# Two chunks of an attention-plus-MLP kernel share each half of the weights, with partial sums in a DRAM scratch

## The chip, the cores and the metric

The kernel runs on one core of a Trainium2 chip. The metric is the device time of one execution in microseconds (us), the median of several runs; lower is better. Engines are named as in the profile: PE (matrix products), PEld (its weight loads), DVE (VectorE), ACT (ScalarE), POOL (GpSimd), SP (SyncE, which issues nearly all DMAs here).

## The reference

Attention with a causal window of 128 keys and 4 sink keys, over 4 batches, 8 heads, 768 positions and 64 channels a head; then a two-layer MLP with a squared ReLU over the 3072 resulting rows of 512 channels:

```python
scores = q @ k.T / sqrt(64)
keep = (pos_k < n_sink) | ((rel >= 0) & (rel < window))     # rel = pos_q - pos_k
a = softmax(where(keep, scores, -1e9)); x = a @ v           # heads side by side: 3072 x 512
r = maximum(x @ w_in, 0)                                    # w_in 512 x 2048
out = (s * (r * r) + b) @ w_out                             # w_out 2048 x 512, float32
```

## The kernel before

*Chunks and weights.* The 3072 rows are cut into eight chunks of 384 rows (half a batch each), taken in the order 0, 2, 1, 3, 4, 5, 6, 7. The 2048 hidden columns are cut into 16 "weights" of 128 columns: `weight[f]` holds the slice of `w_in` and of `w_out` that belongs to them. Products are done in a rounded 32-bit format in three parts: high x high, high x low, low x high. So every operand is split into two halves, and each product is three matmuls.

*The MLP of one chunk* (`moe_steps`) is a list of steps. `l1(f)` multiplies x by the first half of weight f (12 matmuls into one PSUM tile `h`, L569), takes the ReLU on ACT (L572), squares and scales on DVE (L573), and splits the result into the high part (ACT, L575) and the low part (DVE, L576) of a tile `g`, of which there are three buffers. `l2(f)` multiplies `g` by the second half (nine matmuls, L587) and adds into three PSUM tiles `po`, one for each 128 rows, which stay open for all 16 weights. Step `l2(f)` stands two weights behind `l1(f)`. After the last weight ACT scales each `po` into an `ot` tile (L591), and SP stores it (L684).

*Attention for the next chunk* is cut into slots that are dealt out evenly over the steps of the current chunk. For the chunks that stand first in their batch's order (chunk 0, and chunk 2 as the second) the slots come from `plain_slots`: 24 units of scores (L474), row maximum (L481), exponent (L487), normalisation (L494 to L497), transposes (L509), product with v (L522), and the split of x into two tiles (L525, L526). For the others they come from `attn_slots`, which uses `hl` tiles (two buffers, one for each head in flight), `xm` tiles and sink corrections; its last unit writes x at L384 and L385. x has two buffers.

*Making the weights.* The weights arrive as raw 32-bit pairs of 1 MB a weight (L172), or in two pieces (the last weights: L172 and L180), and are turned into the high and low halves by stages: two ACT passes (L199, L200), two DVE passes (L201, L202) and one POOL addition (L204), then an ACT copy (L209), and a subtraction on DVE or, for each fourth weight, on POOL (L215). The raw pieces of the very last weight lie in two buffers of `g`. `weights(n_load, n_make)` issues loads and stages up to a given number; there are 33 stages. A function `before` calls it ahead of each `l1(f)` of the first chunk, with two stages for each weight.

The instructions of all engines are put into order by a scheduler, in which the order of writing is the priority: an instruction that is ready can be placed ahead of an earlier one that is not. Dependencies between tiles are followed by the framework.

Of the kernel before, what the change touches and what calls it, by code (L numbers as in the profile page):

```python
# [6 lines left out]
F32 = mybir.dt.float32  # L7
# [5 lines left out]
ALU = mybir.AluOpType  # L13
AX = mybir.AxisListType

P = 128
B, H, S, D = 4, 8, 768, 64
NS = 16
BLK = 3
CH = BLK * P  # L20
DM = H * D
DFF = 2048
NCC = DM // P
NF = DFF // P
# [3 lines left out]
WUP = 256.0  # L28
LOADS = 8
SMB, HLB = 4, 2  # L30
# [4 lines left out]
ORDER = 0, 2, 1, 3, 4, 5, 6, 7  # L35
LB, LC, LD, L2 = 2, 4, 1, 2
# [3 lines left out]
def tile_kernel(ctx, tc, qT, kT, k0, v, vsk, n_sink, window, w, s, b, out):  # L40
    nc = tc.nc
# [5 lines left out]
    def ps(name):  # L47
        return psA.tile([P, 512], F32, tag="a", name=name)

    wk_cm = tc.tile_pool(name="wk", bufs=2)  # L50
    wk = wk_cm.__enter__()
# [170 lines left out]
    def new_chunk(c):  # L222
        k = Chunk()
        k.c, k.b, k.half = c, c // 2, c % 2
        k.x = [wk.tile([P, NCC, CH], F32R, tag=f"x{i}", name=f"x{i}_{c}") for i in range(2)]
        k.cc, k.xx, k.heads, k.pairs = {}, {}, {}, {}
        return k
# [145 lines left out]
    def unit_d(k, h, i):  # L373

        if h % 2 == 1 and i == BLK - 1:
            pr = h // 2
            pp = k.pairs[pr]
            os_ = ps("os")
            nc.tensor.matmul(os_[:, :CH], pp.vs, pp.xs, start=True, stop=True)
            zb = ps("zb")  # L380
            nc.tensor.matmul(zb[:, :CH], sel, pp.xs, start=True, stop=True)
            nc.vector.tensor_tensor(out=pp.x, in0=os_[:, :CH], in1=pp.x, op=ALU.add)
            nc.vector.tensor_tensor(out=pp.x, in0=zb[:, :CH], in1=pp.x, op=ALU.mult)
            nc.scalar.copy(k.x[0][:, pr, :], pp.x)  # L384
            nc.gpsimd.tensor_tensor(out=k.x[1][:, pr, :], in0=pp.x, in1=k.x[0][:, pr, :].bitcast(F32), op=ALU.subtract)  # L385

    def attn_slots(c):
        k = new_chunk(c)
        units, ahead = [], {}
        for pr in range(H // 2):  # L390
            h, t0 = 2 * pr, 2 * BLK * pr
            units += [(h + hh, i) for hh in range(2) for i in range(BLK)]
            todo = ((-5, load_pair, pr), (-5, load_keys, h), (-2, load_sinks, pr), (-2, prep_head, h), (-2, load_keys, h + 1),
                    (1, prep_head, h + 1))
            for d, fn, a in todo:
                ahead.setdefault(max(t0 + d, 0), []).append((fn, a))
        n = len(units)

        def slot(t):
            def f():  # L400

                for fn, a in ahead.get(t, ()):
                    fn(k, a)
                if t < n:
                    unit_a(k, *units[t])
                if 0 <= t - LB < n:
                    unit_b(k, *units[t - LB])
                if 0 <= t - LC < n:
                    unit_c(k, *units[t - LC])
                if 0 <= t - LC - LD < n:  # L410
                    unit_d(k, *units[t - LC - LD])
            return f

        return k, [slot(t) for t in range(n + LC + LD)]
# [140 lines left out]
        return k, [slot(t) for t in range(n + lc)]  # L555


    def moe_steps(x, store, wk, before=None, last=False):
        g = {}
        po = [None] * BLK  # L560

        def l1(f):
            if before:
                before(f)
            h = ps("h")
            i = 0
            for cc in range(NCC):
                for wi, xi in ((0, 0), (0, 1), (1, 0)):
                    nc.tensor.matmul(h[:, :CH], weight[f][:, 0, wi, cc * P:(cc + 1) * P], x[xi][:, cc, :], start=(i == 0), stop=(i == 11))  # L569
                    i += 1  # L570
            r = wk.tile([P, CH], F32, tag="r", name="r", bufs=RB)
            nc.scalar.activation(r, h[:, :CH], AF.Relu, scale=1.0 / WUP)  # L572
            nc.vector.scalar_tensor_tensor(out=r, in0=r, scalar=s_ap, in1=r, op0=ALU.mult, op1=ALU.mult)  # L573
            gg = wk.tile([P, 2, CH], F32R, tag="g", name="g", bufs=3)
            nc.scalar.activation(gg[:, 0, :], r, AF.Identity, bias=b_ap, scale=1.0)  # L575
            nc.vector.scalar_tensor_tensor(out=gg[:, 1, :], in0=r, scalar=b_ap, in1=gg[:, 0, :].bitcast(F32),  # L576
                                           op0=ALU.add, op1=ALU.subtract)
            g[f] = gg

        def l2(f):  # L580
            gg = g.pop(f)
            for tb in range(BLK):
                if f == 0:
                    po[tb] = psO.tile([P, DM], F32, tag="po", name="po")
                tsl = slice(tb * P, (tb + 1) * P)
                for i, (gi, wi) in enumerate(((0, 0), (0, 1), (1, 0))):
                    nc.tensor.matmul(po[tb], gg[:, gi, tsl], weight[f][:, 1, wi, :],  # L587
                                     start=(f == 0 and i == 0), stop=(f == NF - 1 and i == 2))
                if f == NF - 1:
                    ot = wk.tile([P, DM], F32, name="ot", **(dict(tag="hl", bufs=HLB) if last and tb < 2 else dict(tag="ot")))  # L590
                    nc.scalar.mul(ot, po[tb], 1.0 / WUP)  # L591
                    store(tb, ot)

        steps = []
        for f in range(NF + L2):
            if f < NF:
                steps.append(lambda f=f: l1(f))
            if f >= L2:
                steps.append(lambda f=f: l2(f - L2))
        return steps  # L600

# [79 lines left out]
    def store_at(c):  # L681
        def f(tb, ot):
            r0 = c * CH + tb * P
            nc.sync.dma_start(out[r0:r0 + P, :], ot)  # L684
        return f
# [3 lines left out]
    def weights(n_load, n_make):  # L689
        while made[0] < min(n_make, 2 * NF + 1):  # L690
            while made[0] // 2 >= loaded[0] and loaded[0] < NF:
                load_weight(loaded[0])
                loaded[0] += 1
            make_weight(made[0])
            made[0] += 1

        n_wide = NF - NARROW - 1
        while loaded[0] < min(n_load, NF) and (loaded[0] < n_wide or made[0] > 2 * n_wide - 2):
            load_weight(loaded[0])
            loaded[0] += 1  # L700

    def before(f):
        weights(f + 2 + LOADS // 2, 2 * f + 5)

    def out_of_range():

        bad = const.tile([P, 4], F32, tag="bad", name="bad")
        nc.vector.tensor_reduce(out=bad[:, 0:1], in_=negm, axis=AX.X, op=ALU.max)
        nc.vector.tensor_scalar(out=bad[:, 0:1], in0=bad[:, 0:1], scalar1=0.9e9, scalar2=None, op0=ALU.is_ge)
        tc.keep_in_program_order(nc.vector.tensor_scalar(out=bad[:, 1:2], in0=n_ap, scalar1=float(NS), scalar2=None, op0=ALU.is_gt))  # L710
        nc.vector.tensor_scalar(out=bad[:, 2:3], in0=w_ap, scalar1=float(P), scalar2=None, op0=ALU.is_gt)
        nc.vector.tensor_scalar(out=bad[:, 3:4], in0=w_ap, scalar1=1.0, scalar2=None, op0=ALU.is_lt)
        bad1 = const.tile([P, 1], F32, tag="bad1", name="bad1")
        nc.vector.tensor_reduce(out=bad1, in_=bad, axis=AX.X, op=ALU.max)
        cnt = ps("cnt")
        nc.tensor.matmul(cnt[0:1, 0:1], bad1, one, start=True, stop=True)
        flag = const.tile([1, 1], I32, tag="flag", name="flag")
        nc.vector.tensor_copy(flag, cnt[0:1, 0:1])
        go = nc.values_load(flag, min_val=0, max_val=P)
        return go  # L720

    NC_ = 2 * B
    k, slots = plain_slots(0)
# [8 lines left out]
    first_cm.__exit__(None, None, None)  # L732
    late_cm = tc.tile_pool(name="late", bufs=1)
    late.append(late_cm.__enter__())
    for j, c in enumerate(ORDER):
        steps = moe_steps(k.x, store_at(c), wk, before if j == 0 else None, j == NC_ - 1)
        slots = []
        if j + 1 < NC_:
            k, slots = (plain_slots if j == 0 else attn_slots)(ORDER[j + 1])
        i = 0  # L740
        for n, st in enumerate(steps):
            st()
            if j == NC_ - 1 and n == NF // 2:
                go = out_of_range()
            while i < len(slots) and i * len(steps) < (n + 1) * len(slots):
                slots[i]()
                i += 1

    late_cm.__exit__(None, None, None)
    wk_cm.__exit__(None, None, None)  # L750
    with tc.If(go > 0):
# [46 lines left out]
```

## Time and profile before

| what | value |
|---|---|
| time of three runs | 775.47, 776.76, 777.45 us; median 776.76 |
| the profiled execution | 775.64 us, of which the span of instructions is 773.9 |
| PE busy | 733.9 us, 95% of the span |
| PE weight load, DVE, ACT, POOL busy | 85%, 64%, 62%, 31% |
| mean granted PE clock | 0.989 |
| read from and written to DRAM | 45.88 MB and 6.29 MB |

A busy share is the time in which an engine had an instruction running. DVE's and POOL's instructions can also be busy while they wait for memory. A view by windows gives the busy time of each engine in stretches of the span, a view by lines groups instructions of one source line, engine and shape, with their mean duration and with what ended the idle time ahead of them.

### The profile page before, as it was taken

What the parts mean: (1) busy time and instruction counts of PE and PEld (TensorE: products, weight loads), DVE (VectorE), ACT (ScalarE), POOL (GpSimd) and SP (SyncE); (2) the same over time, 40 slices, a digit from 0 to 9 for tenths busy, and PEclk for the clock granted to TensorE, in tenths of its full rate; (3) what the DMA queues carried; (4) which work ended last, traced back from release to release, by engine and by line L of the source; (5) the groups of instructions that cost most, each with busy time, mean ns of one, the idle gap of its engine ahead of it and who ended that gap; (6) DMA issues with size and microseconds to landing.
All of it is one profiled execution on the core that took longest, in us unless ns stands there. A gap on an engine that the chain in (4) does not pass through costs nothing.

```text
span 773.9 us, 11988 instructions
## 1 busy us (share of the span) xinstructions
PE 733.9 (95%) x4024; PEld 654.0 (85%) x4024; DVE 496.9 (64%) x1222; ACT 477.9 (62%) x1187; POOL 237.0 (31%) x377
## 2 busy tenths in 40 slices
PE   7877788899999999999999999999999999999996
PEld 4565567789999999989989999899989999899895
DVE  7879989636776567656667466765676466653321
ACT  5987658547766567656676566656666576643222
POOL 4134643213333233323333233323243233310000
PEclk9999899999999999999999999999999999999998
DMA  8953042022111221112111212112112212001001
GB/s 185 395 213 136 17 134 66 11 80 67 53 54 54 69 67 45 41 43 88 33 57 55 69 50 57 36 44 79 40 54 58 75 44 58 24 1 42 1 0 46
DMA packets 32309, 53.03 MB, mean 69 GB/s; under 512 B 9840, under 2 KB 20720, under 8 KB 30320
## 3 DMA queue, kind: packets, MB, share of 16 engines
q1 hardware_dynamic: 31152, 51.98, 21.7%
q8 instruction: 34, 0.56, 0.3%
q10 hardware_dynamic: 1088, 0.20, 0.1%
q14 instruction: 35, 0.29, 0.1%
HBM read 45.88 MB, written 6.29 MB: 67 GB/s over the span
## 4 chain that ended last, share of the span: by engine, by line
PE 78%; DVE 9%; ACT 3%; issue 2%; POOL 1%; DMA 1%; ACTq 0%; DVEq 0%; POOLq 0%
PE h L569 32%; PE po L587 30%; PE o L355 5%; PE sc L295 2%; PE sc L294 2%; PE tp L318 2%; DVE w L202 2%; PE tp L317 2%; DVE r L573 1%; DVE w L215 1%; DVE wt L201 1%; DVE sm_p L497 1%; PE o L522 1%; DVE g L576 1%; PE ts L368 1%
## 5 line engine op out<-in xcount | busy, mean ns | idle before, releaser
L569 PE MATMUL h<-x,w 128*128 128x384 f32 x1536 | 299.7, 344 | 3.6 <-ACT w L209 3.3
L587 PE MATMUL po<-w,g 128*128 128x512 f32 x1152 | 297.7, 402 | 5.0 <-DVE g L576 2.6
L569 PEld LDWEIGHTS h<-x,w 128*128 128x128 f32 x1536 | 270.5, 190 | 7.5 <-ACT w L209 3.7
L587 PEld LDWEIGHTS po<-w,g 128*128 128x128 f32 x1152 | 209.5, 189 | 48.0 <-DVE g L576 4.8
L572 ACT ACTIVATE r<-h 128x384 f32<-128x384 f32 x128 | 63.0, 492 | 114.5 <-PE h L569 110.4
L573 DVE SCALAR_TENSOR_TENSOR r<-r,sb 128x384 f32<-128x384 f32 x128 | 88.7, 693 | 55.2 <-ACT r L572 55.2
L576 DVE SCALAR_TENSOR_TENSOR g<-r,sb,g 128x384 fp32r<-128x384 f32 x128 | 82.3, 643 | 47.1 <-ACT g L575 45.2
L299 DVE CUSTOM_DVE_ANT_0 sm<-sc,msk 128x272 f32<-128x272 f32 (+1 forms) x144 | 60.8, 422 | 80.4 <-PE sc L295 65.5
L575 ACT ACTIVATE g<-r,sb 128x384 fp32r<-128x384 f32 x128 | 78.7, 615 | 32.7 <-DVE r L573 31.6
L306 POOL COPY psk<-sm 128x48 f32<-128x48 f32 x144 | 38.3, 266 | 166.0 <-ACT sm L305 164.7
L305 ACT ACTIVATE sm<-sm,negm 128x272 f32<-128x272 f32 (+1 forms) x144 | 73.7, 512 | 20.4 <-DVE negm L299 19.1
L274 POOL TENSOR_TENSOR kl<-kraw,kh 128x544 fp32r<-128x544 f32 (+1 forms) x48 | 61.3, 1278 | 56.3 <-ACT kh L272 50.0
L322 ACT CAST hl<-tp 128x256 fp32r<-128x256 f32 (+1 forms) x144 | 51.3, 356 | 28.7 <-PE tp L318 28.2
L323 DVE TENSOR_TENSOR hl<-tp,hl 128x256 fp32r<-128x256 f32 (+1 forms) x144 | 57.9, 402 | 8.1 <-ACT hl L322 7.3
L355 PE MATMUL o<-hl,vv 128*128 128x256 f32 (+1 forms) x352 | 61.5, 293 | 0.0
L279 POOL TENSOR_TENSOR vv<-vraw,vv 128x256 fp32r<-128x256 f32 (+1 forms) x48 | 34.7, 724 | 59.8 <-ACT vv L278 57.4
L204 POOL TENSOR_TENSOR w<-w 128x1024 int32<-128x1024 int32 (+1 forms) x17 | 33.0, 1946 | 53.8 <-DVE w L202 28.2
L355 PEld LDWEIGHTS o<-hl,vv 128*128 128x128 f32 x352 | 47.9, 190 | 0.5
L364 DVE TENSOR_TENSOR xm<-o,y 64x384 f32<-64x384 f32 x48 | 26.5, 552 | 31.3 <-ACT y L363 31.1
L295 PE MATMUL sc<-kl,qs 128*128 128x272 f32 (+1 forms) x144 | 41.4, 287 | 0.0
L294 PE MATMUL sc<-kh,qs 128*128 128x272 f32 (+1 forms) x144 | 40.4, 280 | 0.0
L318 PE MATMUL tp<-identr,sm 128*128 128x128 f32 x144 | 39.1, 272 | 0.0
(128 smaller groups left out, 885.8 us busy)
## 6 DMA issues: line engine op xcount, KB each, us to landing
w<-in_w SPq DMA_DIRECT2D x15, 1024.0 KB, 8.5
kraw<-in_kT SPq DMA_DIRECT2D x32, 272.0 KB, 2.7
out<-ot SPq DMA_DIRECT2D x24, 256.0 KB, 2.0
qraw<-in_qT SPq DMA_DIRECT2D x24, 192.0 KB, 2.4
vraw<-in_v SPq DMA_DIRECT2D x16, 256.0 KB, 2.8
kraw<-in_kT SPq DMA_DIRECT2D x16, 208.0 KB, 2.4
vsraw<-in_vsk SPq DMA_DIRECT2D x24, 64.0 KB, 1.8
vraw<-in_v SPq DMA_DIRECT2D x8, 192.0 KB, 2.4
```

The lines of the kernel that those rows point to most:

```text
L274: nc.gpsimd.tensor_tensor(out=hd.kl[:, :kw], in0=hd.k[:, :kw], in1=hd.kh[:, :kw].bitcast(F32), op=ALU.subtract)
L295: nc.tensor.matmul(sc[:, :n], hd.qs[:, qs], hd.kl[:, c0:c0 + n], start=False, stop=True)
L299: nc.vector.tensor_tensor_reduce(out=sm[:, :n], in0=sc[:, :n], in1=m, scale=-0.125, scalar=BIG, op0=ALU.add, op1=ALU.min, accum_out=negm[: ...
L305: nc.scalar.activation(sm[:, :n], sm[:, :n], AF.Exp, bias=negm[:, uu], scale=-1.0, accum_out=pp.zz[:, i, hh:hh + 1])
L323: nc.vector.tensor_tensor(out=lo, in0=tp[:, a:z], in1=hi.bitcast(F32), op=ALU.subtract)
L355: nc.tensor.matmul(hd.o[:, q0:q0 + n * P], hd.vv[:, kb, :], hd.hl[:, t, c0 * P:(c0 + n) * P], start=(hd.n == 0), stop=(i == BLK - 1 and kb ...
L569: nc.tensor.matmul(h[:, :CH], weight[f][:, 0, wi, cc * P:(cc + 1) * P], x[xi][:, cc, :], start=(i == 0), stop=(i == 11))
L572: nc.scalar.activation(r, h[:, :CH], AF.Relu, scale=1.0 / WUP)
L573: nc.vector.scalar_tensor_tensor(out=r, in0=r, scalar=s_ap, in1=r, op0=ALU.mult, op1=ALU.mult)
L575: nc.scalar.activation(gg[:, 0, :], r, AF.Identity, bias=b_ap, scale=1.0)
L576: nc.vector.scalar_tensor_tensor(out=gg[:, 1, :], in0=r, scalar=b_ap, in1=gg[:, 0, :].bitcast(F32), op0=ALU.add, op1=ALU.subtract)
L587: nc.tensor.matmul(po[tb], gg[:, gi, tsl], weight[f][:, 1, wi, :], start=(f == 0 and i == 0), stop=(f == NF - 1 and i == 2))
```

## The change

The first two chunks in order (0 and 2) are taken together. Four runs of steps take the place of the first two chunks' lists:

1. a0: chunk 0 with weights 0 to 7, beside all attention slots of chunk 2. Its three sums are scaled by ACT and stored to a DRAM scratch, `part[0]`.
2. a1: chunk 2 with weights 0 to 7, beside no slots. Its sums go to `part[1]`.
3. b0 and b1, one list: chunk 0 with weights 8 to 15, then chunk 2 with weights 8 to 15, beside the attention slots of chunk 1. At the end of each, the saved sum is loaded into a tile `pt`, which takes one of the two `hl` buffers, and DVE adds the scaled new sum to it in one instruction per 128 rows; the result is stored.

The stages of making weights follow: two for each weight in a0, one for each weight in a1 and in b0. The other six chunks run as before. The read of the range flag in the last chunk stands one step earlier.

```diff
-    def moe_steps(x, store, wk, before=None, last=False):
+    def moe_steps(x, store, wk, before=None, last=False, fs=range(NF), part_out=None, part_in=None):
         g = {}
+        f0, f1 = fs[0], fs[-1]
...
                 for i, (gi, wi) in enumerate(((0, 0), (0, 1), (1, 0))):
                     nc.tensor.matmul(po[tb], gg[:, gi, tsl], weight[f][:, 1, wi, :],
-                                     start=(f == 0 and i == 0), stop=(f == NF - 1 and i == 2))
-                if f == NF - 1:
+                                     start=(f == f0 and i == 0), stop=(f == f1 and i == 2))
+                if f == f1 and part_in is not None:
+                    if tb == 0:
+                        pt = wk.tile([P, 2, 2 * CH], F32, name="pt", tag="hl", bufs=HLB)
+                        pt = pt.rearrange("p t c -> p (t c)").rearrange("p (t c) -> p t c", t=BLK)
+                        nc.sync.dma_start(pt, part_in)
+                    nc.vector.scalar_tensor_tensor(out=pt[:, tb, :], in0=po[tb], scalar=1.0 / WUP, in1=pt[:, tb, :],
+                                                   op0=ALU.mult, op1=ALU.add)
+                    store(tb, pt[:, tb, :])
+                elif f == f1:
                     ot = wk.tile([P, DM], F32, name="ot", **(dict(tag="hl", bufs=HLB) if last and tb < 2 else dict(tag="ot")))
                     nc.scalar.mul(ot, po[tb], 1.0 / WUP)
-                    store(tb, ot)
+                    if part_out is not None:
+                        nc.sync.dma_start(part_out[:, tb, :], ot)
+                    else:
+                        store(tb, ot)
...
-    def before(f):
+    def before_a0(f):
         weights(f + 2 + LOADS // 2, 2 * f + 5)
+
+    def before_a1(f):
+        n = NF + 4 + f
+        weights(n // 2 + 4, n)
+
+    def before_b0(f):
+        n = max(2 * f + 5, NF + 4 + f)
+        weights(n // 2 + 4, n)
...
+    part = [part_pool.tile([P, BLK, DM], F32, tag=f"part{i}", name=f"part{i}") for i in range(2)]
+    lo_f, hi_f = range(NF // 2), range(NF // 2, NF)
...
+    k1_, slots = plain_slots(ORDER[1])
+    run(moe_steps(k0_.x, None, wk, before_a0, fs=lo_f, part_out=part[0]), slots)
+    run(moe_steps(k1_.x, None, wk, before_a1, fs=lo_f, part_out=part[1]), [])
+    k, slots = attn_slots(ORDER[2])
+    run(moe_steps(k0_.x, store_at(ORDER[0]), wk, before_b0, fs=hi_f, part_in=part[0]) +
+        moe_steps(k1_.x, store_at(ORDER[1]), wk, fs=hi_f, part_in=part[1]), slots)
+    for j, c in enumerate(ORDER[2:], 2):
...
```

More of the change, by code (lines that the diff above doesn't have):

```diff
@@ L582, in l2 @@
             for tb in range(BLK):
-                if f == 0:
+                if f == f0:
                     po[tb] = psO.tile([P, DM], F32, tag="po", name="po")
@@ L587, in l2 @@
                     nc.tensor.matmul(po[tb], gg[:, gi, tsl], weight[f][:, 1, wi, :],
-                                     start=(f == 0 and i == 0), stop=(f == NF - 1 and i == 2))
-                if f == NF - 1:
+                                     start=(f == f0 and i == 0), stop=(f == f1 and i == 2))
[8 more added lines that the diff above has]
+                elif f == f1:
                     ot = wk.tile([P, DM], F32, name="ot", **(dict(tag="hl", bufs=HLB) if last and tb < 2 else dict(tag="ot")))
                     nc.scalar.mul(ot, po[tb], 1.0 / WUP)
-                    store(tb, ot)
+                    if part_out is not None:
+                        nc.sync.dma_start(part_out[:, tb, :], ot)
+                    else:
+                        store(tb, ot)
         steps = []
-        for f in range(NF + L2):
-            if f < NF:
+        for f in range(f0, f1 + 1 + L2):
+            if f <= f1:
                 steps.append(lambda f=f: l1(f))
-            if f >= L2:
+            if f >= f0 + L2:
                 steps.append(lambda f=f: l2(f - L2))
@@ L734, in tile_kernel, with run @@
     late.append(late_cm.__enter__())
[L735 to L739, printed above, removed]
+    part_cm = tc.tile_pool(name="part", bufs=1, space=bass.MemoryType.DRAM)
+    part_pool = part_cm.__enter__()
+    part = [part_pool.tile([P, BLK, DM], F32, tag=f"part{i}", name=f"part{i}") for i in range(2)]
+    flag_read = []
+    lo_f, hi_f = range(NF // 2), range(NF // 2, NF)
+    def run(steps, slots):
         i = 0
@@ L742, in tile_kernel @@
             st()
-            if j == NC_ - 1 and n == NF // 2:
-                go = out_of_range()
             while i < len(slots) and i * len(steps) < (n + 1) * len(slots):
@@ L747, in tile_kernel, with with_flag @@
                 i += 1
+    k0_ = k
+    k1_, slots = plain_slots(ORDER[1])
[5 more added lines that the diff above has]
+    for j, c in enumerate(ORDER[2:], 2):
+        steps = moe_steps(k.x, store_at(c), wk, None, j == NC_ - 1)
+        slots = []
+        if j + 1 < NC_:
+            k, slots = attn_slots(ORDER[j + 1])
+        if j == NC_ - 1:
+            st = steps[NF // 2]
+            def with_flag():
+                flag_read.append(out_of_range())
+                st()
+            steps[NF // 2] = with_flag
+        run(steps, slots)
+    go = flag_read[0]
+    part_cm.__exit__(None, None, None)
     late_cm.__exit__(None, None, None)
```

## The prediction

> **What bounds the kernel now.** I read the page first: the shares of each engine, then its 40 slices.
>
> ```profile
> span 773.9 us, 11988 instructions
> PE 733.9 (95%) x4024; PEld 654.0 (85%) x4024; DVE 496.9 (64%) x1222; ACT 477.9 (62%) x1187; POOL 237.0 (31%) x377
> ...
> PE   7877788899999999999999999999999999999996
> ...
> DVE  7879989636776567656667466765676466653321
> ```
>
> A slice is 19.3 us. PE is full from the ninth slice on, and before that it has holes while DVE stands at 8 and 9 tenths. So there is a start that is not bound by PE, and a steady part that is. The next view cuts the span at the stages (columns: length; busy us and count of PE, weight load, DVE, ACT, POOL; granted clock, DMA share, GB/s).
>
> ```profile
> 42.00:109.00 67.00, 52.12 (x234) 40.99 (x231) 63.79 (x91) 48.65 (x83) 30.85 (x18) 0.92 0.34 125
> 101.00:169.00 68.00, 58.47 (x281) 47.71 (x280) 47.86 (x96) 39.29 (x91) 23.43 (x22) 0.97 0.23 71
> 42.00:169.00 127.00, 104.85 (x488) 84.52 (x486) 103.65 (x173) 83.40 (x165) 51.72 (x38) 0.95 0.27 93
> 169.00:258.00 89.00, 88.69 (x516) 81.92 (x516) 57.58 (x148) 57.64 (x150) 29.73 (x52) 1.00 0.21 60
> 116.00:140.00 24.00, 21.48 (x109) 17.87 (x110) 21.90 (x50) 19.09 (x46) 10.05 (x10) 1.00 0.19 58
> 700.00:774.00 74.00, 67.68 (x338) 60.58 (x337) 19.95 (x33) 20.25 (x37) 0.71 (x1) 0.97 0.06 23
> ```
>
> The borders come from the PE timeline (first product of the first chunk), the chain of the end (one weight's products) and the DMA queue's timeline (stores of the first and the second chunk):
>
> ```profile
> 42.09 1.30 PE L569 MATMUL h<-x,w 128*128 128x384 f32 x6
> 169.68 4.08 SPq L684 DMA_DIRECT2D out<-ot  x3
> 258.29 3.09 SPq L684 DMA_DIRECT2D out<-ot  x3
> 167.58 2.10 PE po L587 x9
> 169.67 2.12 PE h L569 x12
> ```
>
> The first chunk takes 42.1 to 169.7, 127.6 us; the second 88.6 us, with PE busy in 88.69 of 89. Both do the same products: per weight 2.12 + 2.10 = 4.22 us, for 16 weights 67.5 us, beside the next chunk's attention. What the first has on top is the making of the weights. In its first 67 us DVE is busy 63.79: DVE bounds there. From 101 us on DVE has holes too (47.86 of 68), so short chains between the engines bound it. Stage one loses at least 127 - 104.85 = 22 us of PE, and more inside the rows that are called busy.
>
> **The change part by part.** I call the four runs of steps a0 (first chunk, eight weights), a1 (second chunk, the same eight) and b (the second halves of both, one list). The work of PE is the same; what moves is which attention and which weight-making lie beside it. So the sum is over three stretches, against 127.6 + 88.6 = 216.2 us.
>
> *a0.* It holds half the first chunk's products, all 29 slots of the second chunk's attention (1.8 per step instead of 0.9) and weights made two stages per weight, as before. PE cannot need more than 104.85 - 8 x 4.22 = 71 us. DVE: from its 103.65 us goes what now lies later. Rows of DVE from 101 to 169 us:
>
> ```profile
> L573 DVE SCALAR_TENSOR_TENSOR r<-r,sb 128x384 f32<-128x384 f32 x9 | 8.5, 949 | 4.3 <-ACT r L572 4.3
> L576 DVE SCALAR_TENSOR_TENSOR g<-r,sb,g 128x384 fp32r<-128x384 f32 x10 | 7.3, 727 | 3.0 <-ACT g L575 2.9
> ...
> L215 DVE TENSOR_TENSOR w<-w,w 128x1024 fp32r<-128x1024 f32 x3 | 3.7, 1218 | 2.9 <-ACT w L209 2.9
> ...
> L202 DVE SCALAR_TENSOR_TENSOR w<-w,wt 128x512 int32<-128x512 int32 x4 | 2.7, 684 | 0.0
> L215 DVE TENSOR_TENSOR w<-w,w 128x512 fp32r<-128x512 f32 x4 | 2.7, 678 | 0.0
> ...
> L202 DVE SCALAR_TENSOR_TENSOR wraw<-wraw,wt 128x512 int32<-128x512 int32 x2 | 2.1, 1054 | 0.1
> L273 DVE TENSOR_TENSOR qs<-qraw,qs 64x384 fp32r<-64x384 f32 x2 | 2.1, 1048 | 0.1
> ...
> L526 DVE TENSOR_TENSOR x<-o,x 128x384 fp32r<-128x384 f32 x3 | 1.7, 557 | 3.5 <-ACT x L525 3.4
> ...
> L201 DVE TENSOR_SCALAR wt<-w 128x512 int32<-128x512 int32 x4 | 1.6, 423 | 0.6 <-ACT w L200 0.6
> ...
> L201 DVE TENSOR_SCALAR wt<-wraw 128x512 int32<-128x512 int32 x2 | 0.8, 414 | 0.0
> ```
>
> Out of a0 go eight hidden rows, 8 x (0.949 + 0.727) = 13.4; the three narrow weights, 2.7 + 2.7 + 2.1 + 1.6 + 0.8 = 9.9; three wide subtractions, 3.7; the third chunk's qs, 2.1: together 29.1 by rows. Rows overlap a little (all DVE rows of that stretch add up to 52.7 against 47.86 busy, a factor 0.91), so 26.5. Left: 77.2. Added are the waits that stay:
>
> ```profile
> DVE wt L201 <- PE o L522: 4.6, 1, 4.6
> ACT x L525 <- PE o L522: 3.0, 1, 3.0
> PE tp L509 <- DVE sm_p L497: 10.0, 6, 2.5
> ```
>
> The 4.6 us at the start stays: 81.8, and with a little for the chains I take **83 us**. Low end: the wide conversions of weights 10 to 12 are now written into a1, though before their kind ran early; by the rows of 42 to 109 us they are 3 x (0.847 + 1.303) = 6.5:
>
> ```profile
> L202 DVE SCALAR_TENSOR_TENSOR w<-w,wt 128x1024 int32<-128x1024 int32 x11 | 14.3, 1303 | 0.0
> L573 DVE SCALAR_TENSOR_TENSOR r<-r,sb 128x384 f32<-128x384 f32 x8 | 12.0, 1494 | 0.2 <-ACT r L572 0.2
> ...
> L201 DVE TENSOR_SCALAR wt<-w 128x1024 int32<-128x1024 int32 x11 | 9.1, 847 | 4.6 <-PE o L522 4.6
> ```
>
> which gives 76. High end: the whole 10.0 us for which the transposes waited for DVE come on top, 92. I stay near DVE's own sum, because in 42 to 109 us, the stretch most like a0, DVE is 95% busy.
>
> *a1.* Eight weights' products, 8 x 4.22 = 33.8, no attention, one making stage per weight. It begins with the last quarter of x, where ACT waited 3.0 for the last attention product; nine of the first twelve products don't need it, so I add 2: **36 us**. The loads of the last weights start here, once stage 25 is made; before, one such load held the chain:
>
> ```profile
> 104.28 4.71 DMA w<-in_w
> ```
>
> If that stays, 36 + 4.7 = 41. Floor 33.8.
>
> *b.* It is the old second chunk's 88.6 us plus what is new. (1) The last narrow weights and the six additions that replace six ACT scalings. An addition reads PSUM as L526 does (557 ns for 384 columns), so 557 x 512 / 384 = 743 ns, 4.5 us in all; with the 9.9 of the narrow weights DVE has 57.58 + 14.4 = 72 of 89 us: hidden under PE. ACT's 24 scalings stay 24 (two 600 ns rows merely move). (2) The raw pieces of the last weight hold two of the three buffers of `g` from a1's sixth weight to b's sixth, nine weights; before, the same squeeze lay in 116 to 140 us, where PE was still busy 21.48 of 24, so 10%; over some 20 us of it in b, 2 us, between 0 and 5. (3) Each saved sum `pt` lies in one of the two `hl` buffers of the attention. Its life is a load of 768 KB, three additions and a store:
>
> ```profile
> w<-in_w SPq DMA_DIRECT2D x15, 1024.0 KB, 8.5
> out<-ot SPq DMA_DIRECT2D x24, 256.0 KB, 2.0
> wraw<-in_w SPq DMA_DIRECT2D x2, 512.0 KB, 3.8
> ```
>
> Between 3.8 and 8.5 by size that is 6.1, with 2.2 and 2.0 some 10.3 us. A head holds its buffer for five slots of 88.6 / 29 = 3.06 us, 15 of the 18 us of two heads, so `pt` pushes one head back by up to 10.3 - 3 = 7 us. Matrix products of the MoE are there to run meanwhile; I take 2, between 0 and 7. The last `pt` comes when the heads are through. (4) The third chunk's x takes the first chunk's buffer, whose last reader is step 13 of b's 32; its first writer belongs to slot 11, after step 12. That is about one step late; `xm` has two buffers, and only ACT's L384 and POOL's L385 stand behind it: 0. So b is 88.6 + 4 = **92.6 us**, from 88.6 to 101.
>
> *The queues.* Six more stores of 256 KB and two loads go through SP, which issued three stores in 4.08 us; at the end of a0 and a1 only weight loads and the third chunk's first keys stand behind them. The partial sum is read two stretches after its store, far above the few us of a landing: no wait. POOL issues the same. The PSUM for the next half is free after three scalings or additions (about 2 us), and three first products (6.4 us) come before it is asked for. The flag's read stands one step earlier in the last chunk, where DVE is busy 19.95 of 74 us: 0.
>
> *The sum:* 83 + 36 + 92.6 = 211.6 against 216.2: 4.6 us less. The profiled execution took 775.64 (span 773.9 and 1.7 around it), which makes 771.0; its median over three runs is 776.76, so on that scale **772 us**.
>
> A rule of the Trainium skill speaks to the same rows: "TensorE: Matmul & The Clock Gate", section "Why this matters for your kernels", says that idle gaps of PE over about 3 us bring the half clock back; its "Part 1" gives the window as 3.4 us. The trace agrees as far as the granted clock goes: 0.92 in 42 to 109 us, 1.00 in 169 to 258. By it the bubble ahead of a1 would cost up to half of a further 3.4 us window, and the sum would be 773 to 774; without it, 772.
>
> **The rivals.** *The full gain.* If a0 keeps only its own weights (76), a1 runs at PE's pace (34) and b hides all (89.6), the three make 199.6: 16.6 less, about 760. For it: PE waits almost nowhere in 169 to 258 with DVE at 65%. Against: weight-making ran ahead of its turn before (all eleven wide conversions were done by 109 us, when eight weights were used), and it will again.
>
> *The attention eats it.* Attention at twice the rate beside weight-making lengthens a0 to 88 by its chains, and the rest is as forecast: 216.6, no change, 777. For it: L573 took 1494 ns in 42 to 109 us and 949 later; POOL was busy 30.85 of 67 there. The Trainium skill's "GPSIMD Engine Reference", section "Key points", says POOL shares its SBUF interfaces with DVE instructions that read two SBUF inputs, which fits these two durations.
>
> *Slower: the `hl` buffer.* If the `pt` in the middle of b holds the attention back for its whole life and nothing fills it, and its late heads then hold the third chunk's start, b takes 88.6 + 2 + 10.3 + 4 (the landing of the queue's stores ahead of it, two of 2.0) = 105; the three make 224, 7.8 more: 784.5. It decides from about 7 us of lost PE time on. For it: buffers are held 15 of 18 us. Against: PE in b always has products of the other chunk in its order.
>
> **How the numbers follow.** The forecast 45% (own range 765 to 777), the full gain 17%, eaten 19%, slower 19%. A difference under 0.3% (2.3 us) can't be told from none here. The forecast's range falls below 774.4 in about nine of ten; with the full gain faster has 0.58, no change 0.21, slower 0.21. The range 761 to 784 leaves out the tips of the full gain and of the slower case.
>
> **What would show it.** The first partial store should be issued near 125 us and the second near 161; the second chunk's final stores near 254 instead of 258.3. In a0 DVE should be busy over 90%, in a1 PE over 90%; b should keep PE at 95% or more. Wrong if a0 ends after 130, if PE waits in b for `hl` or `g` by several us, or if weight 13's load holds ACT in a1.

## The result, and the profile after

The changed kernel takes 789.38 us (median of four runs, 788.07 to 789.77) against 776.81 for the kernel before in the same comparison: a ratio of 1.0169, interval 1.0155 to 1.0183. It is slower. The forecast was 772, faster, with a range of 761 to 784.

The head of the page after:

```profile
span 788.0 us, 12025 instructions
PE 743.4 (94%) x4024; PEld 660.9 (84%) x4024; DVE 499.8 (63%) x1228; ACT 479.9 (61%) x1187; POOL 237.4 (30%) x377
...
PE   7877679997989999999999999999999999999997
...
DVE  7879984528667676764676567764667567663221
```

The work is the same (PE's 4024 matmuls, ACT's 1187 instructions; DVE has six more), and the span is 14.1 us longer. The slices show three dips of PE where before there was one long start. The borders of the stages, from the PE timeline (a1's first products) and the DMA queue's (a1's partial stores, the second chunk's final stores):

```profile
137.12 6.61 PE L572 MATMUL h<-x,w 128*128 128x384 f32 x36
173.86 3.60 SPq L604 DMA_DIRECT2D part<-ot  x3
273.18 1.53 SPq L698 DMA_DIRECT2D out<-pt  x3
```

a0 begins at 42.1 as the first chunk did before. So:

| stretch | forecast | measured |
|---|---|---|
| a0 | 83 | 95.0 |
| a1 | 36 | 36.7 |
| b | 92.6 | 99.3 |
| sum (before: 216.2) | 211.6 | 231.0 |

The stages as windows of the changed kernel (columns as in the prediction):

```profile
42.00:109.00 67.00, 47.70 (x189) 36.02 (x188) 61.29 (x90) 47.57 (x82) 32.19 (x21) 0.82 0.34 125
109.00:137.00 28.00, 26.74 (x134) 20.73 (x133) 16.59 (x51) 22.42 (x58) 6.81 (x9) 1.00 0.29 86
42.00:137.00 95.00, 74.44 (x321) 56.75 (x320) 77.89 (x140) 70.00 (x139) 39.00 (x29) 0.87 0.33 113
137.00:174.00 37.00, 36.02 (x181) 31.99 (x180) 14.95 (x23) 14.07 (x27) 3.32 (x3) 1.00 0.18 58
174.00:220.00 46.00, 41.73 (x225) 37.75 (x224) 35.27 (x80) 29.41 (x75) 22.57 (x30) 0.93 0.18 53
220.00:247.00 27.00, 24.24 (x135) 22.61 (x134) 18.30 (x44) 16.05 (x44) 9.42 (x17) 0.94 0.36 117
```

a0 falls into two parts. Until 109 us DVE is full (61.29 of 67) and PE has holes; from 109 on PE is full (26.74 of 28) and DVE stands at 16.59 of 28. The two engines take turns. The rows of the first part, DVE's of the changed kernel and PE's of the changed and of the earlier one, show what fills it:

```profile
L202 DVE SCALAR_TENSOR_TENSOR w<-w,wt 128x1024 int32<-128x1024 int32 x11 | 15.0, 1367 | 0.0
...
L201 DVE TENSOR_SCALAR wt<-w 128x1024 int32<-128x1024 int32 x11 | 10.2, 946 | 4.6 <-PE o L522 4.6
L576 DVE SCALAR_TENSOR_TENSOR r<-r,sb 128x384 f32<-128x384 f32 x5 | 6.0, 1209 | 0.6 <-ACT r L575 0.6
```

```profile
L572 PE MATMUL h<-x,w 128*128 128x384 f32 x62 | 13.9, 370 | 0.0
```

```profile
L569 PE MATMUL h<-x,w 128*128 128x384 f32 x96 | 21.8, 377 | 3.3 <-ACT w L209 3.3
```

All eleven wide conversions run in the first 67 us, as they did before, though three of them are written into a1. Then five weights of MLP had passed DVE in the changed kernel instead of eight: 62 first products instead of 96. In b there are two holes. The first lies where the last narrow weights are made beside the first heads (PE's and POOL's timeline), the second where the saved sum is loaded (chain of the end, waits, PE's timeline). PE waits 2.97 us in the first and 2.76 in the second:

```profile
192.44 1.18 PE L590 MATMUL po<-w,g 128*128 128x512 f32 x2 [2.97 <-DVE g L579]
192.04 3.08 POOL L215 TENSOR_TENSOR w<-wraw,w 128x512 fp32r<-128x512 f32 x2 [0.60 <-ACT w L209]
```

```profile
220.86 6.33 DMA pt<-part
DVE pt L597 <- DMA pt<-part: 4.9, 1, 4.9
229.67 0.30 PE L317 MATMUL tp<-identr,sm 128*128 128x128 f32 x1 [2.76 <-DVE negm L299]
```

In the first, DVE makes narrow weights (L215, up to 191.13) between the high part of a `g` tile, which ACT wrote from 188.04 to 188.68, and its low part (L579, from 191.78), for which PE waits; and the next high part waits for POOL's L215, which reads one of the raw pieces that lie in `g` buffers:

```profile
189.01 2.12 DVE L215 TENSOR_TENSOR w<-w,w 128x512 fp32r<-128x512 f32 x2
193.58 0.62 ACT L578 ACTIVATE g<-r,sb 128x384 fp32r<-128x384 f32 x1 [0.58 <-POOL w L215]
```

In the second, the addition stands at the head of DVE's order and waits 4.9 us for its load; the row maximum queued behind it is what PE then waits for.

### The profile page after: what moved, and what is told of

Read it like the earlier page. It is cut to its first block, busy times and chain, and to the rows that moved or that the text cites. A ratio compares the mean times of both kernels' runs of the same rounds, so it can differ in the third digit from the quotient of the medians.

```text
span 788.0 us, 12025 instructions
## 1 busy us (share of the span) xinstructions
PE 743.4 (94%) x4024; PEld 660.9 (84%) x4024; DVE 499.8 (63%) x1228; ACT 479.9 (61%) x1187; POOL 237.4 (30%) x377
## 4 chain that ended last, share of the span: by engine, by line
PE 77%; DVE 11%; ACT 6%; POOL 2%; DMA 2%; issue 1%; SPq 0%; ACTq 0%; POOLq 0%; DVEq 0%
PE h L572 32%; PE po L590 29%; PE o L355 4%; PE sc L295 2%; PE sc L294 2%; PE tp L318 2%; PE tp L317 2%; DVE w L202 1%; DVE w L215 1%; DVE r L576 1%; DVE wt L201 1%; POOL w L204 1%; DVE g L579 1%; DVE sm_p L497 1%; PE ts L368 1%
## 5 line engine op out<-in xcount | busy, mean ns | idle before, releaser
L576 DVE SCALAR_TENSOR_TENSOR r<-r,sb 128x384 f32<-128x384 f32 x128 | 83.5, 652 | 64.2 <-ACT r L575 64.1
L579 DVE SCALAR_TENSOR_TENSOR g<-r,sb,g 128x384 fp32r<-128x384 f32 x128 | 83.0, 648 | 51.0 <-ACT g L578 48.8
L295 PE MATMUL sc<-kl,qs 128*128 128x272 f32 (+1 forms) x144 | 41.5, 288 | 0.0
```

The costliest lines, as they stand in the source:

```text
L295: nc.tensor.matmul(sc[:, :n], hd.qs[:, qs], hd.kl[:, c0:c0 + n], start=False, stop=True)
```

## The experiments

Theory A to begin with: a0 is long because the making of later weights is placed into it; rival B: attention at twice the rate, by its own chains. For b: theory C (narrow weights) and E (the load of `pt`), with rivals D and F. Four kernels first; each time is the median beside the kernel before on the same chip (775.82). Stages are taken from the profiled run of each; a0 is counted from its first product, which lies between 40.0 and 43.8 us.

**Making held back.** Every making instruction from stage 19 on is pinned:

```diff
+        pin = tc.keep_in_program_order if j >= 19 else (lambda i: i)
-                nc.scalar.activation(lo, lo.bitcast(U32), AF.Copy, scale=2.0 ** -29)
+                pin(nc.scalar.activation(lo, lo.bitcast(U32), AF.Copy, scale=2.0 ** -29))
...
```

> The changed kernel, with every making instruction from stage 19 on (all that is written into a1 and b) pinned behind what is written before it on its engine; so none of them can be placed into a0. Nothing is left out. Theory A (a0 takes 95 us because the scheduler still places the eleven wide conversions into its first 67 us, where DVE is full, and leaves DVE half idle behind): a0 falls by 7 to 12 us to 83 to 88 with DVE idle under 10 us in it, a1 stays within 3 us of 37, and the time falls from 789.4 to 778 to 783. Rival B (attention at twice the rate is what stretches a0, by its chains): a0 stays at 92 to 95, and the time at 786 to 791.

787.57 us (783.96 to 787.96), ratio 1.0149 (1.0132 to 1.0167). The profiled run, the fastest of the five, shows a1's beginning and the two groups of stores:

```profile
128.38 6.60 PE L573 MATMUL h<-x,w 128*128 128x384 f32 x36
170.76 0.82 SPq L605 DMA_DIRECT2D part<-ot  x2
266.67 1.92 SPq L699 DMA_DIRECT2D out<-pt  x3
42.00:131.00 89.00, 73.24 (x332) 57.90 (x331) 65.22 (x132) 56.48 (x123) 30.97 (x25) 0.90 0.31 104
```

a0 (from 41.5) is 86.9, in A's range. The rest of A fails: DVE idles some 24 of 89 us there, where A gave it under 10; a1 grew to 42.4, more than A allowed; and the time fell far less than forecast, by 1.8 us in the medians and by 5.8 in the profiled runs. Three wide weights cost a0 about 8 us, and moving their making out pays part of that in a1.

**All making in a1.**

```diff
-        n = NF + 4 + f
+        n = 2 * NF - 11 + 2 * f
```

> The changed kernel, with two making stages per weight in a1 instead of one, so that all 33 stages are written into a1 and none into b. Nothing is left out. Theory C (b's first hole, near 188 to 201 us, comes from the narrow weights being made on DVE and POOL beside the first heads of the third chunk, 3.0 + 0.9 + 0.4 us of PE waits and 3.4 us lost to the half clock): the hole goes, a1 stays under 39 us, the time is 781 to 784. Rival D (the raw pieces of the last weight then hold two of three g buffers in a1, which pays what b gains): a1 is 41 to 45 us, and the time 787 to 791.

784.59, ratio 1.0115 (1.0092 to 1.0137): 0.6 us above theory C's range, and well below D's. b (175.96 to 267.16) is 91.2 instead of 99.3, and PE is busy 90.58 of 92 in it; a1 is 37.7. The hole goes, as C says. The same edit also takes the raw pieces of the last weight out of b's `g` buffers, so the run doesn't tell what each of the two is worth.

```profile
175.96 3.08 SPq L604 DMA_DIRECT2D part<-ot  x3
267.16 1.53 SPq L698 DMA_DIRECT2D out<-pt  x3
176.00:268.00 92.00, 90.58 (x523) 83.10 (x523) 61.22 (x154) 58.20 (x152) 32.64 (x54) 1.00 0.28 85
```

**No saved sum.** The branch with `part_in` is taken out.

> The changed kernel without the use of the saved sums: the second halves end like any chunk (ACT scales, SP stores), with no load of pt, no hl buffer for it and no DVE addition. This leaves out the first halves' part of the first two chunks' outputs. Theory E (DVE waits 4.9 us in its order for the load of pt in the middle of b, and the PE wait of 2.8 us and a 3.4 us stretch of half clock near 230 us follow from it): these go, and the time is 784 to 786. Rival F (the load's wait only takes up slack, b is long for other reasons): 788 to 790.

786.84, ratio 1.0135 (1.0117 to 1.0153). The time is 0.8 us above what E gave; b is 95.2, so `pt` costs it 4.1 us (2.5 in the whole time), and the first hole stays (3.0 us of PE waiting for DVE's g).

```profile
175.11 3.60 SPq L596 DMA_DIRECT2D part<-ot  x3
270.35 3.12 SPq L690 DMA_DIRECT2D out<-ot  x3
```

**Three edits together.** Pinned, two stages per weight in a1, and `pt` in three pieces:

```diff
+                saved[tb] = wk.tile([P, DM], F32, name="pt", tag="ot")
+                nc.sync.dma_start(saved[tb], part_in[:, tb, :])
```

> The changed kernel with three edits together: making instructions from stage 19 on pinned, two stages per weight in a1, and the saved sums loaded in three pieces of 256 KB into the ot buffers, two of them one weight ahead of their use, instead of one hl buffer at the time of use. Nothing is left out. If theories A, C and E hold and add up (10, 7 and 4 us), 768 to 774, which is faster than the kernel before (776.8). If only A holds: 777 to 783. If none: 786 to 791.

785.03, ratio 1.0124 (1.01 to 1.0147): not additive, and between the forecasts for A alone (777 to 783) and for none (786 to 791). The windows of a1 and b:

```profile
128.00:183.00 55.00, 47.14 (x224) 40.09 (x223) 38.47 (x49) 32.59 (x57) 20.23 (x15) 0.97 0.24 82
183.00:274.00 91.00, 88.68 (x511) 81.14 (x510) 65.65 (x155) 58.53 (x153) 35.58 (x55) 1.00 0.29 90
```

a0 is 87.0, but a1, with six weights to finish and pieces of b's work that slipped into it, is 53.5, and PE is idle for 7.9 of 55 us there.

Next, the order inside a0, its clock, and the kernel before (776.2 in this comparison).

**Attention late in a0.** `run` deals the slots out over the last 10 steps.

> The changed kernel with the second chunk's attention slots dealt out over the last 10 of a0's 16 steps instead of all 16; the making of weights is written as in the changed kernel. Theory A2 (while DVE is full, an attention unit gives PE less work per DVE time than an MLP weight, 3.3 us per 2.8 against 4.2 per 1.2, so a0 loses by having attention and making in the same first 67 us): a0 falls from 95 to 85 to 90, the time to 780 to 785. Rival B (attention in a0 is bound by its own chain, so a later start makes a later end): a0 is 95 to 102 and the time 789 to 796.

787.71, ratio 1.0145 (1.0116 to 1.0174). a0 doesn't shrink: its last partial store is issued at 138.7 instead of 136.6. A2 fails as written, and the time lies below rival B's range too; the order of writing hardly moves a0.

**Idle matmuls in a0.**

> The changed kernel with four idle matmuls of 512 columns (no result used) written ahead of each second-layer step of a0, 32 in all, about 7 us of PE work, to keep PE's clock up; nothing is left out. Theory G (the 24 us at half clock inside a0 lengthen the chains that DVE and ACT wait for, and so cost time): half-clock time in a0 falls under 10 us and a0 shrinks by 4 to 8 us, the time to 782 to 786. Rival H (the half clock only marks the holes, since DVE is the bound there): a0 stays or grows by up to 7, the time is 789 to 797.

792.01, ratio 1.0202 (1.0174 to 1.0229). a0 (41.7 to 141.6) is 100.0. But the granted clock did not rise (0.87 in 42 to 137 us, as in the changed kernel), so the run shows the price of 32 matmuls and leaves theory G undecided:

```profile
42.00:137.00 95.00, 76.66 (x328) 58.42 (x327) 76.40 (x140) 68.04 (x135) 39.07 (x28) 0.87 0.32 111
```

**The kernel before with late attention.**

> The kernel before (not the changed one) with the second chunk's attention slots dealt out over the last 24 of the first chunk's 32 steps. By theory A2 the first chunk loses less, since the first 67 us hold making and MLP alone: first stores at 162 to 168 instead of 169.7, time 769 to 775. By rival B, where the attention's own chain counts, it ends later: 776 to 782.

776.77, ratio 0.9999 (0.9986 to 1.0012): no difference. The first stores begin at 166.7 instead of 169.7, in A2's range, but the second ones at 257.4 instead of 258.3, and the time stays. A2's gain doesn't last.

**Late attention and all making in a1.**

> The changed kernel with late slots in a0 (as in the run with late slots alone) and with two making stages per weight in a1. If the gains of the two add up (4 to 9 us in a0, 5 us in b): 775 to 780, level with the kernel before. If the gain in a0 only moves the making into a1: 782 to 786.

780.53, ratio 1.0051 (1.0033 to 1.007), just above the range for gains that add up. a0's last partial store is at 138.8, so a0 gains nothing; a1 and b gain:

```profile
173.69 3.10 SPq L604 DMA_DIRECT2D part<-ot  x3
264.19 1.53 SPq L698 DMA_DIRECT2D out<-pt  x3
```

b is 90.5. It is the best order found for the changed kernel with its instructions as they are, still slower than before. So I asked what a0 costs without either of its two loads (one profiled run each; the kernel before took 775.81 beside them).

**No making.**

> The changed kernel with the making of weights 2 to 15 left out (loads stay; weights 0 and 1 are used again and again instead, so the output is not the reference's). Theory M (making is what costs PE: a0's holes, 95 - 64 = 31 us for eleven wide weights in the changed kernel and 86 - 64 = 22 for eight in the pinned one, are 2.8 us per wide weight, whatever stands beside it): a0 is 64 to 69 us, a1 34 to 36, b 89 to 94, the time 748 to 757. Rival B (the attention at double rate makes the holes by its own chain): a0 stays over 78 us, the time over 762.

749.99, in theory M's range. a0 is 63.9 (43.6 to 107.5; M gave 64 to 69), with PE busy 66.95 of 68: the attention at double rate leaves almost no holes by itself. Rival B is out.

```profile
107.53 6.60 PE L575 MATMUL h<-x,w 128*128 128x384 f32 x36
42.00:110.00 68.00, 66.95 (x343) 54.65 (x342) 33.20 (x111) 36.66 (x105) 8.46 (x16) 1.00 0.49 167
```

**No attention.**

> The changed kernel without the second chunk's attention (the second chunk uses the first chunk's x, so half of the first two chunks' output is wrong); all making stays as written. PE has 33.8 us of MLP and 3.7 us of leftovers in a0. Theory M: the holes stay at about 31 us, a0 is 65 to 72, the time 760 to 768. Rival B (attention's chain makes the holes): a0 is 40 to 50, the time 738 to 748. Rival S (neither alone: the sum of both on DVE and ACT is what counts, and making alone hides beside the MLP but for DVE's own time of some 44 us and the waits at the start): 48 to 58, the time 747 to 755.

755.95. a0 is 57.6 (42.0 to 99.65): rival S, not M, though the time was a little above its range. DVE's rows and the window:

```profile
42.00:98.00 56.00, 42.90 (x173) 34.68 (x172) 52.97 (x43) 40.05 (x51) 30.75 (x12) 0.86 0.32 127
...
L202 DVE TENSOR_SCALAR wt<-w 128x1024 int32<-128x1024 int32 x10 | 13.9, 1420 | 4.6 <-PE o L523 4.6
...
L580 DVE SCALAR_TENSOR_TENSOR g<-r,sb,g 128x384 fp32r<-128x384 f32 x8 | 12.0, 1494 | 0.0
```

Making and MLP alone fill DVE to 95%, and PE still idles for 13 of the 56 us. DVE does it with few instructions: 43, some of them at more than twice their quiet duration (g: 1494 ns against 624 for the same row, L576, in 169 to 258 us before). POOL is busy 30.75 of the 56 us there. Hence the last question: is DVE at work, or standing still beside POOL's additions?

The timelines of the kernel before answer in part. In its first chunk the squaring (L573) took 606 to 619 ns in the eight cases with no addition or subtraction of POOL beside it, and 1210 to 2764 in the eight with one:

```profile
59.34 2.21 POOL L204 TENSOR_TENSOR w<-w 128x1024 int32<-128x1024 int32 x1
59.72 2.25 DVE L573 SCALAR_TENSOR_TENSOR r<-r,sb 128x384 f32<-128x384 f32 x1
75.47 0.62 DVE L573 SCALAR_TENSOR_TENSOR r<-r,sb 128x384 f32<-128x384 f32 x1
```

Instructions with one tensor input lengthen too (L497, 128x256: 347 against 1450 ns); the row maxima of 128x384, which read PSUM, do not (548 against 550). Set against the mean of the same shape with POOL idle, DVE's rows hold some 28 us more in the first chunk and some 20 in a0 (an estimate, summed over the two traces).

As a test, POOL's additions were folded into DVE's shift:

```diff
-                nc.vector.tensor_scalar(out=t, in0=hi, scalar1=3, scalar2=None, op0=ALU.logical_shift_left)
+                nc.vector.scalar_tensor_tensor(out=t, in0=hi, scalar=3, in1=lo, op0=ALU.logical_shift_left, op1=ALU.bitwise_or)
-                nc.gpsimd.tensor_tensor(out=hi, in0=hi, in1=lo, op=ALU.add)
```

> The kernel before (not the changed one) with POOL's addition of the low bits (L204) folded into DVE's shift: one two-input instruction (shift left, or) takes the place of DVE's shift and POOL's addition; a low part that rounds up to 8 no longer carries. DVE's own work rises by about 0.56 us per wide weight, 6 us in the first chunk. Theory P (DVE is full in the making stretch because its two-input instructions stand still beside POOL's additions, some 24 us of them): the first chunk shortens by 6 to 14 us, first stores at 156 to 164, time 762 to 770. Rival Q (DVE's own instruction work is what counts): first stores at 170 to 176, time 776 to 783.

755.65 against 776.99, ratio 0.9729 (0.971 to 0.9749): theory P, and more than it forecast. The first chunk ends at 149.4 instead of 169.7 (starting 1.4 us earlier).

```profile
149.38 4.18 SPq L683 DMA_DIRECT2D out<-ot  x3
237.98 3.09 SPq L683 DMA_DIRECT2D out<-ot  x3
42.00:109.00 67.00, 59.72 (x290) 49.41 (x291) 61.49 (x112) 56.56 (x106) 11.34 (x12) 0.97 0.42 152
L572 DVE SCALAR_TENSOR_TENSOR r<-r,sb 128x384 f32<-128x384 f32 x10 | 6.4, 645 | 0.1
```

DVE is about as full in 42 to 109 us (61.49 against 63.79), but holds ten weights of MLP there instead of eight; their squaring takes 645 ns instead of 1494. POOL is down from 30.85 to 11.34.

> The changed kernel with the same folding. Theory P: a0 falls from 95 to 80 to 88 and b's first hole shrinks, the time is 771 to 781, and the gap to the folded kernel before stays over 5 us. Rival Q: a0 95 to 101, time 788 to 796.

771.81, ratio 0.994 (0.9916 to 0.9963).

```profile
125.56 6.61 PE L571 MATMUL h<-x,w 128*128 128x384 f32 x36
161.35 3.60 SPq L603 DMA_DIRECT2D part<-ot  x3
254.52 1.53 SPq L697 DMA_DIRECT2D out<-pt  x3
42.00:109.00 67.00, 50.60 (x235) 40.34 (x234) 61.26 (x114) 54.57 (x105) 12.16 (x13) 0.95 0.40 145
```

a0 (from 40.0) is 85.5, a1 35.8, b 93.2. DVE is full for the same 61 of 67 us as in the folded kernel before, but PE gets 50.60 us of work from it instead of 59.72.

> The changed kernel with late slots in a0, two making stages per weight in a1, and the same folding. Theory P: 764 to 774; if it comes out below the folded kernel before, the sharing of weights pays once the making is cheaper. Rival Q: 780 to 787.

763.55, ratio 0.9823 (0.9807 to 0.984): just under P's range of 764 to 774, and still 7.9 us behind the folded kernel before, the fastest of those that leave nothing out.

## Why the prediction was wrong

*a0, the step that failed.* DVE's sum was right: 77.2 forecast, 77.89 measured. Wrong was what I put beside it, 5.8 us of idle DVE, "because in 42 to 109 us, the stretch most like a0, DVE is 95% busy". That was the first part of a stage. Measured, DVE idled for 17.1 us of a0, and the stage ended at 137, past the 130 that I had named as a sign of being wrong. Over the whole first chunk before, DVE had been busy 103.65 of 127, or 82%; with that share 77.2 gives 94 to 95 us, and 77.89 of 95 is again 82%. Part of that agreement is luck: in the pinned kernel the share is 73%. Making comes first and fills DVE, then PE is left with the rest while DVE idles. The low end for early conversions was no low end: all eleven ran early again. Theory A holds only for a0's length, as the pinned kernel showed. What each load costs is shown by leaving out one at a time: 63.9 us without making and almost no holes, 57.6 without attention and still 13 us of holes in 56, 95.0 with both. So making, not attention, opens the holes, and both together stretch the stage. That much of DVE's time was standing still beside POOL is shown by the durations and by the folding. A small slip: the DVE rows of 101 to 169 us add up to 53.9 us, not 52.7, which makes DVE's sum 77.8.

*What the sum hid.* Eight weights of MLP went out of a0. They took 33.8 us of PE work along, but only 13.4 us of DVE rows. A stretch bound by DVE gets shorter by the second number, and PE loses the work that had filled its holes. In a1 that work stands without making beside it: DVE is busy 14.95 of 37 there. This reading is argued, not shown: it fits the windows of the two folded kernels, 59.72 against 50.60 us of PE at equally full DVE; it was not tested by itself, and the runs with late attention, which should have gained by it, didn't in a0.

*a1* was right (36 and 36.7); the load of the narrow weights did not hold it, and PE's clock was 1.00, so there was no stretch at half clock.

*b.* Item 1, narrow weights "hidden under PE", failed: with all making in a1, b lost 8.1 of its 99.3 us, and the trace shows DVE at L215 while PE waits. The mean load of 72 us in 89 hid that the making falls together at b's start. Item 2, the squeeze of g, has no price of its own in the runs: moving the making moved the squeeze with it, and a1 with both was 1 us longer; in b, ACT's g waited 0.58 us for it. Item 3 was mis-sized and misplaced: 4.1 us instead of 2, and in the trace not as a head that the `hl` buffer holds back but by DVE's order, in which the addition waits for a load of 6.33 us (6.1 forecast) and holds the next row maximum. I had not named what is queued behind the addition. Item 4 was right: ACT waited 1.4 us for the third chunk's x, and PE not at all.

*The rivals.* The nearest was attention eating the gain, by its place (a0), but at 88 us instead of 95. The slower rival had the right side and the wrong mechanism. The full gain needed making to be free; without making the kernel does run at 750.

*The two rules.* The granted clock was 0.87 in a0 and 1.00 in a1. That is what "TensorE: Matmul & The Clock Gate" of the Trainium skill (section "Why this matters for your kernels") says of holes (PE's longest waits in a0 were 3.3 to 3.9 us); whether the half clock cost time or only marked the holes stays open, since the idle matmuls did not raise it. The "GPSIMD Engine Reference" of the Trainium skill (section "Key points") says that POOL shares its SBUF interfaces with VectorE, in "contention with DVE instructions in a 2-port perf mode or with two SBUF inputs"; the folded kernel before agrees (1494 against 645 ns for the squaring, which has two such inputs). I had weighed it as a rival's detail, but taking POOL's additions away took 17.6 us off the changed kernel (789.38 to 771.81).

## What to carry to other kernels

When work is moved out of a stage, count what each engine loses: a stage bound by one engine should shrink by what is moved off that engine, and the rest is only filler taken away (argued above, not tested by itself). To price a rebuilt stage, divide its busy sum by the share that the whole old stage reached, not by that of its fullest part; take it as a rough guide, since holding back three conversions moved the share from 82% to 73%. And look at durations before moving work: an instruction at twice its quiet duration points at a neighbour, here POOL, and removing that neighbour was worth 21 us where the rearrangement cost 13.

## What the runs showed of the hardware that I had not expected

POOL's additions of the making took some 24 us in a0, and DVE instructions beside POOL's took far longer than their quiet duration (the squaring up to 2764 ns instead of 606 to 619), while the row maxima, which read PSUM, did not. In the kernel before, folding the additions into DVE, which gave DVE about 0.53 us more work of its own per wide weight (1216 ns for the new shift against 684 for an undisturbed old one), shortened the first chunk from 127.6 to 108.7 us. And 32 more matmuls, written ahead of a0's second-layer steps, left the granted clock where it was, 0.87.
